# The opening loads of a fused attention and feed-forward kernel: batch 0's state block in one load with the first half of x, the first quarter of w_in as whole blocks, its stores issued by GpSimd

## The chip, the cores and the metric

The kernel runs on one core of one Trainium2 chip. The metric is the device time of one execution in microseconds (us). Three executions of the kernel before took 629.32, 629.43 and 630.81 us, so the median is 629.43 us. TensorE is called PE here, VectorE DVE, ScalarE ACT, GpSimd POOL and SyncE SP.

## The reference

Eight batches of eight heads attend between 512 rows of x and 32 rows of a state, in both directions. The result, 4608 rows of 512 numbers, goes through a feed-forward block whose activation is `h - tanh(h)`.

```python
scores = scale * x @ state.T;  a = softmax(scores);   xread = a @ state
scores2 = scale * state @ x.T; a2 = softmax(scores2); sread = a2 @ x
rows = concatenate([xread, sread])         # B, H, 544, 64 -> 4608 rows of 512
h = rows @ w_in                            # 512 x 2048
out = (h - tanh(h)) @ w_out                # 2048 x 512
```

The inputs x, state, `w_in` and `w_out` arrive as numpy arrays. The two weights are 64-bit floats: the kernel loads them as pairs of 32-bit words and makes 32-bit floats of them on the chip. The rest is 32-bit.

## The kernel before

**Stages.** Work goes chunk by chunk, one chunk for each batch and a last one for the state rows. Within a chunk the hidden layer is made in 16 slices of 128 columns, and each slice is multiplied with its rows of `w_out`. The product state times `w_in` is taken first (called m in the code), so that the attention weights can be multiplied with m directly and the read of the state needs no step of its own. Batch 0 has a hand-written opening, which is what the change touches. The others come from generators that a list of due steps drives.

**The opening.** Its order is written out in the string `SEQ` (line 821): each token is one step, and `tc.keep_in_program_order` holds the steps of an engine in this order. The steps that matter here:

- `D`: a matmul of zeros on PE (line 720). Five stand at the start.
- `S0`, `S1` (line 724): the scores of half 0 and half 1 of x for batch 0. Two matmuls each, of the state block with the two column groups of that half.
- `c0`, `c1` (line 729): ACT copies the scores out of PSUM. `T0`, `T1` (line 735): PE transposes them.
- `M0`, `B0`, `E0`, `Z0`, `z0`, `q0`, `N0` (lines 738 to 753): the softmax of half 0, all on DVE but the exponential `E0` on ACT. `A0` (line 758) transposes the result back on PE.
- `bj`, `aj`, `rj`, `pj` (lines 136 to 139): the four steps that turn a weight block from 64 into 32 bits. `b` and `a` run on DVE, `r` on ACT, `p` on DVE again. j counts the four blocks of the first quarter of `w_in` (tiles w00 to w03), each 128 columns wide, then two row blocks of `w_out`.
- After `pj` of the first four blocks, the converted block is stored to the buffer `wf` in device memory (line 777), from which the other batches read it much later.
- `mj` multiplies block j with the state of batches 0 and 1, `hj` and `Hj` are the first hidden slices.

DVE's order begins `b0 a0 M0 B0 p0 Z0 b1 a1 z0 p1 q0 a2 b2 N0 p2`.

**The loads.** SP issues nearly all transfers, in the order of the program, on one queue (q1 in the profile). Before the first step the code issues: `x00`, the state block with the first column group of half 0 (128 rows of 3 KB); from ACT, on a second queue (q10), the second column group of half 0 (128 rows of 2 KB); then from SP w00, half 1 of x, `sps` (another layout of the state, 256 KB), w01, w02, w03 and two blocks of `w_out`. Each further weight block is loaded when a conversion frees its buffer; that is `load(1)` in the step `p`. The blocks w00 to w03 are 128 columns of all 512 rows of `w_in`: a row of the tile is four pieces of 1 KB from four places.

The lines with which the opening sets its loads up:

```python
xb = big("x00", [P, 768], F32)
xrs = [pool.tile([P, 2, 512], F32, tag="x", name=f"xT0{hf}", bufs=XB) for hf in range(2)]
nc.sync.dma_start(xb, x0)
nc.scalar.dma_start(xrs[0][:, 1], xT[0, 0][:, 1])
load(1)
nc.sync.dma_start(xrs[1], xT[0, 1])
nc.sync.dma_start(sps, sp[0])
load(4)
```

`pooled(dst, src)` (line 300) issues a transfer from GpSimd, in the order of such calls. GpSimd's queue otherwise begins its transfers at 87.67 us, with the reads of `wf`.

Of the kernel before, what the change touches and what calls it, by code (L numbers as in the profile page):

```python
# [20 lines left out]
P = 128  # L21
# [4 lines left out]
NQ = 4  # L26
# [9 lines left out]


@with_exitstack
def attention_ffn(ctx: ExitStack, tc: tile.TileContext, xT, xn, x0, bh, sp, sm, win, wout, xout, tout, sout):

# [54 lines left out]
    def big(name, shape, dtype):  # L97
        return pool.tile(shape, dtype, tag="big", name=name, bufs=BIG)
# [7 lines left out]
    class Weight:  # L106
# [2 lines left out]
        def __init__(self, src, name):  # L109
            self.src, self.name = src, name  # L110

        def load(self):
            if self.src.dtype == F32:
                self.raw = next(raws)(f"{self.name}d", [P, 512], F32)
                dst = self.raw
            else:
                self.raw = next(raws)(f"{self.name}d", [P, 512, 2], U32)
                dst = self.raw.rearrange("p f w -> p (f w)")
            src = self.src.bitcast(dst.dtype)
            if len(src.shape) == 3:  # L120
                dst = dst.rearrange("p (r f) -> p r f", r=4)
            loadlog.append(nc.sync.dma_start(dst, src).ins)

        def steps(self, dst):

# [516 lines left out]
    def advance(units, n=1):  # L642
# [5 lines left out]


    w0 = [  # L650
        [Weight(win[r * P : r * P + P, 512 * q : 512 * q + 512], f"w{q}{r}") for r in range(DM // P)]
        for q in range(NQ)
    ]

    w0[0] = [
        Weight(win[:, j * P : j * P + P].rearrange("(r p) f -> p r f", p=P), f"w0{j}") for j in range(4)
    ]
    wos = [Weight(wout[f * P : f * P + P], f"wo{f}") for f in range(NFF)]
    wfs = {}

    def convert_win(q, p):
        if p % 2 == 0:
            wfs[q, p // 2] = pool.tile([P, 2, 512], F32, tag="wf", name=f"w0{q}{p // 2}", bufs=WB)
        made = w0[q][p].convert(wfs[q, p // 2][:, p % 2])
        if p % 2:
            nc.sync.dma_start(wf[q][:, p - 1 : p + 1], wfs[q, p // 2])
        return made
# [22 lines left out]

    aTs[0] = pool.tile([P, 2, 2, 512], F32R, tag="aT0", name="aT0", bufs=1)
    sps = pool.tile([P, 4, P], F32, tag="sm", name="sps", bufs=1)
    xb = big("x00", [P, 768], F32)
    xrs = [pool.tile([P, 2, 512], F32, tag="x", name=f"xT0{hf}", bufs=XB) for hf in range(2)]
    nc.sync.dma_start(xb, x0)
    nc.scalar.dma_start(xrs[0][:, 1], xT[0, 0][:, 1])
    load(1)
    nc.sync.dma_start(xrs[1], xT[0, 1])
    nc.sync.dma_start(sps, sp[0])
    load(4)  # L700
    bdr = xb[:, :256].rearrange("p (i m) -> p i m", i=4)
    moving = {(0, 0): xb[:, 256:]} | {(j, c): xrs[j][:, c] for j, c in ((0, 1), (1, 0), (1, 1))}

    warm = bank(ps_a, "warm")
    m_first[0] = pool.tile([P, 2, 512], F32, tag="mr", name="mr00", bufs=RRB)
# [11 lines left out]
    def step(op):  # L717
        k, j = op[0], int(op[1]) if len(op) > 1 else 0
        if k == "D":
            o(nc.tensor.matmul(warm[:, :256], blank[:, :P], blank, start=True, stop=True))  # L720
        elif k == "S":
            sps_ps[j] = bank(ps_o, f"sps0{j}")
            for c in range(2):
                o(nc.tensor.matmul(sps_ps[j][64 * c : 64 * c + 64], bdr[:, 2 * j + c], moving[j, c], start=True, stop=True))
        elif k == "c":
            if j == 0:
                kept[0] = pool.tile([P, 2, 512], F32, tag="g", name="s0", bufs=GB)
            ss[j] = kept[0][:, j]
            o(nc.scalar.copy(ss[j], sps_ps[j]))
        elif k == "T":  # L730

            tps[j] = bank(ps_o, f"tps0{j}")
            for t in range(4):
                cols = slice(P * t, P * t + P)
                o(nc.tensor.transpose(tps[j][:, cols], ss[j][:, cols], ident))
        elif k == "M":
            ms[j] = pool.tile([P, 16, 1], F32, tag="m1", name=f"m10{j}")
            o(nc.vector.reduce_max(ms[j], tps[j].rearrange("p (a n) -> p a n", n=32), axis=AX.X))
        elif k == "B":
            es[j] = pool.tile([P, 512], F32, tag="e", name=f"e0{j}")  # L740
            s3 = tps[j].rearrange("p (a n) -> p a n", n=32)
            o(nc.vector.tensor_sub(e3(j), s3, ms[j].broadcast_to([P, 16, 32])))
        elif k == "E":
            o(nc.scalar.activation(es[j], es[j], AF.Exp, scale=SCALE))
        elif k == "Z":
            zs[j] = pool.tile([P, 16, 1], F32, tag="z", name=f"z0{j}")
            o(nc.vector.reduce_sum(zs[j], e3(j), axis=AX.X))
        elif k == "z":
            o(nc.vector.tensor_scalar_add(zs[j], zs[j], EPS))
        elif k == "q":  # L750
            o(nc.vector.reciprocal(zs[j], zs[j]))
        elif k == "N":
            o(nc.vector.tensor_mul(e3(j), e3(j), zs[j].broadcast_to([P, 16, 32])))
        elif k == "A":
            aps[j] = bank(ps_o, f"aps0{j}")
            for t in range(4):
                cols = slice(P * t, P * t + P)
                o(nc.tensor.transpose(aps[j][:, cols], es[j][:, cols], ident))
        elif k == "y":
            ats[j] = pool.tile([P, 512], F32, tag="p2t", name=f"at0{j}", bufs=PTB)  # L760
            o(nc.scalar.copy(ats[j], aps[j]))
        elif k in "abrp":
            if j not in csteps:
                if j > 3:
                    if j == 4:
                        plain[0] = big("wp0", [P, 2, DM], F32)
                    csteps[j] = wos[j - 4].steps(plain[0][:, j - 4])
                else:
                    if j % 2 == 0:
                        wb[j // 2] = pool.tile([P, 2, 512], F32, tag="wf", name=f"w00{j}", bufs=WB)  # L770
                    csteps[j] = w0[0][j].steps(wb[j // 2][:, j % 2])
            o(csteps[j]["abrp".index(k)]())
            if k == "p":
                load(1)
            if k == "p" and j < 4:
                w = wb[j // 2][:, j % 2].rearrange("p (r f) -> p r f", r=4)
                nc.sync.dma_start(wf[0][:, :, j * P : j * P + P], w)
        elif k == "m":
            w = wb[j // 2][:, j % 2].rearrange("p (r f) -> p r f", r=4)
            if j >= APART:  # L780
                mps[j] = bank(MP[j], f"mps0{j}").rearrange("p (r f) -> p r f", r=4)
                for p in range(4):
                    o(nc.tensor.matmul(mps[j][:, p], sps[:, p], w[:, p], start=True, stop=True))
                return

            mps[j] = bank(MP[j], f"mps0{j}").rearrange("p (b k f) -> p b k f", b=2, k=2)
            for p in (0, 2):
                for b in range(2):
                    for c in range(2):
                        rows = slice(64 * c, 64 * c + 64)  # L790
                        cols = slice(64 * b, 64 * b + 64)
                        o(nc.tensor.matmul(mps[j][rows, b, p // 2], sps[:, p + c, cols], w[:, p + c], start=True, stop=True))
        elif k in "kR":
            b = "kR".index(k)
            if b and 0 not in m_second:
                m_second[0] = second(0)
            cols = slice(j * P, j * P + P)
            if j < APART:
                o(nc.scalar.copy((m_first, m_second)[b][0][:, :, cols], mps[j][:, b]))
                return  # L800
            for c in range(2):
                rows = slice(64 * c, 64 * c + 64)
                o(nc.scalar.copy((m_first, m_second)[b][0][rows, :, cols], mps[j][64 * b : 64 * b + 64, c::2]))
        elif k in "hH":
            if k == "h":
                hps[j] = bank(ps_h if j > 1 else ps_o, f"hps0_{j}")
            i = "hH".index(k)
            o(nc.tensor.matmul(hps[j], m_first[0][:, i, j * P : j * P + P], ats[i], start=(i == 0), stop=(i == 1)))  # L808
        elif k == "X":
            t = hts[j] = pool.tile([P, 512], F32, tag="t", name=f"t0_{j}", bufs=TB)  # L810
            hts[j, 0] = nc.scalar.activation(t, hps[j], AF.Tanh)
            o(hts[j, 0])
        elif k == "x":
            g = chunks[0].g[j] = pool.tile([P, 512], F32, tag="g", name=f"g0_{j}", bufs=GB)
            d = nc.vector.tensor_sub(g, hps[j], hts[j])
            o(d)
            tanhs.append((hts[j, 0].ins, d.ins))
# [9 lines left out]
    turn = firstDVE[0]  # L827
    for p in range(2):
        with tc.issue_after(turn):
            turn = convert_win(1, p)  # L830
        load(1)
        m_first_two(1, p)

# [510 lines left out]
```

## Time and profile before

| what | value |
|---|---|
| median of three executions | 629.43 us |
| the profiled execution | 629.0 us |
| its span, first to last instruction | 627.2 us |
| around the span | 1.8 us |
| PE busy | 621.5 us, 99% |
| DVE, ACT, POOL busy | 78%, 59%, 6% |
| granted PE clock over the span | 0.999 |
| bytes moved | 155.9 MB, mean 249 GB/s |

The share of busy time is a mean over the whole span. PE's 99% contain the matmuls of zeros of the opening and matmuls whose modelled end includes a wait, so the first 14 us have to be read by themselves: by the chain that ended last, the waits and the order of time.

### The profile page before, as it was taken

The numbers are of one execution on the slowest core, as the hardware profiler recorded it, in microseconds if no ns is written. First come the engines' busy times: TensorE is split into PE (matmuls) and PEld (weight loads), VectorE is DVE, ScalarE is ACT, GpSimd is POOL, SyncE is SP. The second block draws the span as 40 slices with busy tenths as digits, with TensorE's granted clock in tenths as the row PEclk, the third lists the DMA queues.
The fourth block names the chain that finished last, engine by engine and source line by source line (L and its number), as shares of the span: only waits on it lengthen the run. The fifth ranks groups of instructions, "written<-read, shape, count | busy, mean of one in ns | idle before, by whom it ended". The sixth has DMA issues, their size and how long they took to land.

```text
span 627.2 us, 9849 instructions
## 1 busy us (share of the span) xinstructions
PE 621.5 (99%) x3610; PEld 490.9 (78%) x3610; DVE 488.8 (78%) x781; ACT 370.4 (59%) x613; POOL 38.7 (6%) x66
## 2 busy tenths in 40 slices
PE   8999999999999999999999999999999999999997
PEld 5456677788888788778886678788888888888997
DVE  5999998799697696998357679988955878764582
ACT  5876777678666475755346785447555543562642
POOL 0000002132311000000000000000000000010000
PEclk9999999999999999999999999999999999999999
DMA  9993875869988857999716996765555675699990
GB/s 318 354 390 135 302 245 145 256 194 341 291 278 287 280 177 262 319 315 397 253 34 217 338 345 212 228 209 168 176 168 183 201 187 164 201 260 341 410 337 26
DMA packets 68672, 155.90 MB, mean 249 GB/s; under 512 B 6032, under 2 KB 27920, under 8 KB 68624
## 3 DMA queue, kind: packets, MB, share of 16 engines
q1 hardware_dynamic: 62400, 134.04, 63.7%
q0 software_dynamic: 6080, 20.98, 11.5%
q8 instruction: 28, 0.46, 0.3%
q10 hardware_dynamic: 144, 0.26, 0.1%
q14 instruction: 20, 0.16, 0.1%
HBM read 110.69 MB, written 44.56 MB: 248 GB/s over the span
## 4 chain that ended last, share of the span: by engine, by line
PE 96%; DVE 2%; ACT 1%; issue 0%; ACTq 0%
PE X L1067 14%; PE hps L553 10%; PE hps L554 10%; PE hps L555 10%; PE ops L606 8%; PE ops L608 8%; PE ops L607 8%; PE Y0m L1067 5%; PE Y1m L1067 5%; PE mps L263 2%; PE mps L179 2%; PE X L1173 2%; PE ops L604 2%; PE Y8m L1173 1%; PE rps L501 1%; PE hps L808 1%
## 5 line engine op out<-in xcount | busy, mean ns | idle before, releaser
L606 PE MATMUL ops<-wo,g 128*128 128x512 f32 x244 | 95.5, 396 | 0.0
L607 PE MATMUL ops<-wo,g 128*128 128x512 f32 x244 | 95.2, 390 | 0.0
L553 PE MATMUL hps<-aT,m 128*128 128x512 f32 x240 | 94.7, 397 | 0.0
L554 PE MATMUL hps<-aT,m 128*128 128x512 f32 x240 | 93.8, 391 | 0.1
L555 PE MATMUL hps<-aT,m 128*128 128x512 f32 x240 | 93.8, 391 | 0.0
L608 PE MATMUL ops<-wo,g 128*128 128x512 f32 x244 | 88.3, 393 | 0.0
L568 ACT ACTIVATE t<-hps 128x512 f32<-128x512 f32 x64 | 38.4, 601 | 57.9 <-PE hps L555 57.2
L568 DVE TENSOR_TENSOR G<-hps,t 128x512 f32<-128x512 f32 x64 | 43.8, 687 | 36.8 <-ACT t L568 36.7
L606 PEld LDWEIGHTS ops<-wo,g 128*128 128x128 f32 x244 | 45.7, 188 | 15.6 <-issue 1.9
L553 PEld LDWEIGHTS hps<-aT,m 128*128 128x128 f32 x240 | 45.0, 188 | 14.5 <-issue 2.5
L580 DVE TENSOR_TENSOR t<-hps,t 128x512 f32<-128x512 f32 x61 | 41.7, 683 | 18.4 <-ACT t L580 18.0
L104 ACT CAST g<-t 128x512 fp32r<-128x512 f32 x61 | 37.8, 619 | 28.5 <-DVE t L580 27.9
L608 PEld LDWEIGHTS ops<-wo,g 128*128 128x128 f32 x244 | 45.6, 188 | 10.8 <-DVE wo L104 0.8
L555 PEld LDWEIGHTS hps<-aT,m 128*128 128x128 f32 x240 | 45.0, 188 | 11.0 <-issue 1.7
L607 PEld LDWEIGHTS ops<-wo,g 128*128 128x128 f32 x244 | 45.8, 188 | 9.9 <-DVE wo L104 0.3
L554 PEld LDWEIGHTS hps<-aT,m 128*128 128x128 f32 x240 | 45.1, 188 | 9.7 <-DVE aT L104 0.5
L580 ACT ACTIVATE t<-hps 128x512 f32<-128x512 f32 x61 | 36.4, 597 | 26.3 <-PE hps L555 25.9
L1067 PE MATMUL X<-g0m,W0m 128*128 128x512 f32 x192 | 47.9, 390 | 0.0
L104 DVE TENSOR_TENSOR g<-t,g 128x512 fp32r<-128x512 f32 x61 | 41.6, 684 | 7.1 <-ACT g L104 6.9
L1067 PE MATMUL X<-g1m,W1m 128*128 128x512 f32 x192 | 45.8, 389 | 0.0
L104 ACT CAST g1m<-G 128x1024 fp32r<-128x1024 f32 x28 | 29.2, 1056 | 27.6 <-PE Y1m L1067 10.9
L1067 PEld LDWEIGHTS X<-g0m,W0m 128*128 128x128 f32 x192 | 36.0, 188 | 8.3 <-issue 0.8
(279 smaller groups left out, 1155.4 us busy)
## 6 DMA issues: line engine op xcount, KB each, us to landing
w<-wf POOLq DMA_DIRECT2D x32, 256.0 KB, 6.5
mm<-st POOLq DMA_DIRECT2D x16, 512.0 KB, 6.3
xn<-in_xn SPq DMA_DIRECT2D x16, 512.0 KB, 5.8
mr<-mm SPq DMA_DIRECT2D x16, 512.0 KB, 5.1
wsd<-ws SPq DMA_DIRECT2D x16, 512.0 KB, 7.7
wod<-wo SPq DMA_DIRECT2D x32, 256.0 KB, 6.6
W0m<-wsd SPq DMA_DIRECT2D x16, 512.0 KB, 3.7
W1m<-wsd SPq DMA_DIRECT2D x16, 512.0 KB, 3.9
```

The lines of the kernel that those rows point to most:

```text
L104: return nc.scalar.copy(hi, src), (sub or nc.vector).tensor_sub(lo, src, hi)
L179: made = nc.tensor.matmul(pss[b][rows], sp2[r, p + c, 64 * b + at : 64 * b + at + 32], w[r, c], start=True, stop=True,)
L553: nc.tensor.matmul(ps, mhi[k][:, cols], ahi[:, k], start=(k == 0), stop=False)
L554: nc.tensor.matmul(ps, mhi[k][:, cols], alo[:, k], start=False, stop=False)
L555: made = nc.tensor.matmul(ps, mlo[k][:, cols], ahi[:, k], start=False, stop=(k == nk - 1))
L568: main(nc.scalar.activation(t, ps, AF.Tanh), nc.vector.tensor_sub(g, ps, t))
L580: tanhs.append((nc.scalar.activation(t, ps, AF.Tanh).ins, nc.vector.tensor_sub(t, ps, t).ins))
L606: nc.tensor.matmul(o, g[:, 0, tok], w[:, 0], start=(f in self.begins), stop=False)
L607: nc.tensor.matmul(o, g[:, 0, tok], w[:, 1], start=False, stop=False)
L608: return nc.tensor.matmul(o, g[:, 1, tok], w[:, 0], start=False, stop=stop).ins
L1067: made = nc.tensor.matmul(out[t], w[:, e, x, cols], y[:, e], start=first and j == 0 and e == 0 and c == 0, stop=last and j == 3 and e == 1 ...
L1173: made = nc.tensor.matmul(out, o[:, x, s], w[:, y], start=first and jp == 0 and s == 0 and c == 0, stop=last and jp == 1 and s == 3 and c ...
```

## The change

It alters four things in the opening, all of them in what is loaded and stored and by which queue.

1. `x00` becomes one tile of 128 rows of 5 KB: the state block and both column groups of half 0. It is loaded by one transfer from SP. The transfer of the second column group from ACT is gone. The tile lies in the buffer `aT1` instead of in one of the sixteen `big` ones, and one buffer of the kind `x` stays free.
2. The first quarter of `w_in` comes as an input of its own, `w0b`, laid out in four whole blocks on the host. A load of w00 to w03 is now 128 rows of 4 KB. The rest of `w_in` is an array of 1536 columns.
3. w00 is issued by ACT instead of by SP, as ACT's first instruction.
4. The four stores of the converted blocks to `wf` are issued by GpSimd with `pooled` instead of by SP.

The scores of half 1 take a PSUM bank of another pool. The code also gains a branch for a step of index 6, which begins the next quarter's first block early; the string `SEQ` is the same as before and names no such step, so nothing takes that branch.

```diff
-        def load(self):
+        def load(self, queue=nc.sync):
...
-            loadlog.append(nc.sync.dma_start(dst, src).ins)
+            loadlog.append(queue.dma_start(dst, src).ins)
...
-    w0[0] = [
-        Weight(win[:, j * P : j * P + P].rearrange("(r p) f -> p r f", p=P), f"w0{j}") for j in range(4)
-    ]
+    w0[:0] = [[
+        Weight(w0b[j], f"w0{j}") for j in range(4)
+    ]]
...
-    xb = big("x00", [P, 768], F32)
-    xrs = [pool.tile([P, 2, 512], F32, tag="x", name=f"xT0{hf}", bufs=XB) for hf in range(2)]
+    xb = pool.tile([P, 1280], F32, tag="aT1", name="x00", bufs=1)
+    xr = pool.tile([P, 2, 512], F32, tag="x", name="xT01", bufs=XB)
     nc.sync.dma_start(xb, x0)
-    nc.scalar.dma_start(xrs[0][:, 1], xT[0, 0][:, 1])
-    load(1)
-    nc.sync.dma_start(xrs[1], xT[0, 1])
+    next(loads).load(nc.scalar)
+    nc.sync.dma_start(xr, xT[0, 1])
...
-            sps_ps[j] = bank(ps_o, f"sps0{j}")
+            sps_ps[j] = bank((ps_o, ps_h)[j], f"sps0{j}")
...
-                nc.sync.dma_start(wf[0][:, :, j * P : j * P + P], w)
+                pooled(wf[0][:, :, j * P : j * P + P], w)
...
-    x0 = c(np.concatenate([bd[0].reshape(P, 256), xT[0, 0, :, 0]], axis=1))
+    x0 = c(np.concatenate([bd[0].reshape(P, 256), xT[0, 0].reshape(P, 2 * S)], axis=1))
...
+    w0b = c(win[:, :512].reshape(4, P, 4, P).transpose(2, 1, 0, 3).reshape(4, P, 512))
+    win = c(win[:, 512:])
```

What the two programs issue at the start, on SP (an arrow points from what is read to what is written; `in_x` are the inputs of x, `in_w` is `w0b`, `wf` the store of a converted block). Before:

```order
L695 DMA x_101<-in_x 128x768
L122 DMA w00d<-in_win 128x4x256
L698 DMA xT_103<-in_xT 128x1024
L699 DMA sps<-in_sp 128x512
L122 DMA w01d<-in_win 128x4x256
L122 DMA w02d<-in_win 128x4x256
L122 DMA w03d<-in_win 128x4x256
L122 DMA wo0d<-in_wout 128x1024
L122 DMA wo1d<-in_wout 128x1024
L122 DMA w10d<-in_win 128x1024
L777 DMA wf_95<-w_125 512x1x128
L122 DMA w11d<-in_win 128x1024
```

SP after:

```order
L693 DMA x_101<-in_x 128x1280
L695 DMA xT_102<-in_xT 128x1024
L696 DMA sps<-in_sp 128x512
L120 DMA w01d<-in_w 128x1024
L120 DMA w02d<-in_w 128x1024
L120 DMA w03d<-in_w 128x1024
L120 DMA wo0d<-in_wout 128x1024
L120 DMA wo1d<-in_wout 128x1024
L120 DMA w10d<-in_win 128x1024
L120 DMA w11d<-in_win 128x1024
```

The first load grew from 768 to 1280 words a row, w00 is gone from behind it, and the store of the first block no longer stands between w10 and w11.

On ACT, before, from its first instruction:

```order
L696 DMA xT_102<-in_xT 128x512
L729 ACT_TABLE_LOAD
L729 COPY s_133<-sps_128 128x512
L138 ACTIVATE w00r<-w00d 128x512
L744 ACTIVATE e_147<-e_147 128x512
```

ACT after:

```order
L120 DMA w00d<-in_w 128x1024
L726 ACT_TABLE_LOAD
L726 COPY s_131<-sps_126 128x512
L136 ACTIVATE w00r<-w00d 128x512
L741 ACTIVATE e_145<-e_145 128x512
```

ACT issues w00 in the place where it issued the second column group of x; its other instructions stand as before.

On GpSimd, before, from the making of the identity matrix to the first reads of `wf`:

```order
masks.py:197 MEMSET ident 128x128
masks.py:199 ISA
masks.py:199 AFFINE_SELECT ident<-ident 128x128
L246 DMA w_1023<-wf_95 64x2x512 x2
L246 DMA w_1063<-wf_95 64x2x512 x2
```

GpSimd after:

```order
masks.py:197 MEMSET ident 128x128
masks.py:199 ISA
masks.py:199 AFFINE_SELECT ident<-ident 128x128
L305 DMA wf_95<-w_123 512x1x128 x2
L305 DMA wf_95<-w_181 512x1x128 x2
L244 DMA w_1021<-wf_95 64x2x512 x2
L244 DMA w_1061<-wf_95 64x2x512 x2
```

The four stores stand ahead of the reads of `wf`. On DVE and PE the two programs hold the same instructions in the same order; on PE both matmuls of `S0` now read the one tile `x00`.

## Rows read from the trace of the kernel before

**Rows 1.** The page: each engine's busy time, share of the span, instructions.

```profile
PE 621.5 (99%) x3610; PEld 490.9 (78%) x3610; DVE 488.8 (78%) x781; ACT 370.4 (59%) x613; POOL 38.7 (6%) x66
```

**Rows 2.** The chain that ended last, 0 to 14 us: start, length, what.

```profile
5.31 1.16 PE sps L724 x4
...
7.23 0.64 PE tps L735 x4
...
7.90 0.70 DVE m L738
...
13.02 0.58 DVE e L753
...
13.73 0.30 PE aps L758
```

**Rows 3.** Busy time by stretch: start:end, length, each engine's busy time (instructions), clock.

```profile
12.00:14.00 2.00, 1.36 (x19) 1.15 (x20) 2.00 (x6) 1.24 (x2) 0.00 (x0) 1.00 1.05 402
14.00:16.00 2.00, 2.00 (x14) 1.46 (x13) 2.00 (x5) 2.00 (x6) 0.00 (x0) 1.00 1.01 392
```

**Rows 4.** Waits for transfers, 0 to 40 us: total, times, longest.

```profile
DVE w00r L137 <- DMA w00d<-in_win: 7.0, 1, 7.0
...
ACT w03r L138 <- DMA w03d<-in_win: 0.7, 1, 0.7
...
PEld sps L724 <- DMA x<-in_x: 0.6, 1, 0.6
```

**Rows 5.** The opening in order of time: start, length, engine, line, operation.

```profile
0.74 0.40 ACTq L696 DMA_DIRECT2D xT<-in_xT  x1
...
5.24 0.64 PE L724 MATMUL sps<-x 128*64 128x512 f32 x1
...
5.39 0.64 PE L724 MATMUL sps<-xT,x 128*64 128x512 f32 x1
...
6.99 0.47 DVE L137 TENSOR_SCALAR w00r<-w00d 128x512 uint16<-128x512 uint16 x1 [6.99 <-DMA w00d<-in_win]
...
7.35 0.41 DVE L136 TENSOR_SCALAR w<-w00d 128x512 uint32<-128x512 uint32 x1
...
10.01 0.69 DVE L747 TENSOR_REDUCE z<-e 128x16 f32<-128x512 f32 x1
...
10.61 0.46 DVE L137 TENSOR_SCALAR w01r<-w01d 128x512 uint16<-128x512 uint16 x1
...
12.12 0.25 DVE L751 RECIPROCAL z<-z 128x16 f32<-128x16 f32 x1
12.23 0.54 SPq L777 DMA_DIRECT2D wf<-w  x1
...
23.59 0.41 DVE L136 TENSOR_SCALAR w<-w10d 128x512 uint32<-128x512 uint32 x1
```

**Rows 6.** Packets by queue, 3 to 4 us: packets, MB, share of 16 engines.

```profile
q1 hardware_dynamic: 74, 0.21, 58.1%
q10 hardware_dynamic: 72, 0.14, 42.5%
```

**Rows 7.** All packets, 5 to 6 us and then 6 to 7 us.

```profile
DMA packets 273, 0.36 MB, mean 363 GB/s; under 512 B 9, under 2 KB 243, under 8 KB 273
DMA packets 140, 0.40 MB, mean 398 GB/s; under 512 B 15, under 2 KB 34, under 8 KB 140
```

**Rows 8.** Stores from SP, 0 to 30 us: count, size, median us from issue to landing.

```profile
wf<-w SPq DMA_DIRECT2D x4, 256.0 KB, 7.7
```

**Rows 9.** GpSimd's transfers, by form: busy us in all, mean ns to issue one.

```profile
L246 POOL DMA_DIRECT2D w<-wf x32 | 19.2, 606 | 127.9 <-DMA smr<-in_sm 86.4 <-DVE wst L249 41.4
L266 POOL DMA_DIRECT2D mm<-st x16 | 11.7, 734 | 48.7 <-ACT st L228 48.7
```

**Rows 10.** DVE beside GpSimd's first transfers, in order of time.

```profile
87.67 1.32 POOL L246 DMA_DIRECT2D w<-wf  x2 [86.36 <-DMA smr<-in_sm]
...
88.39 0.42 DVE L136 TENSOR_SCALAR wor<-wo13d 128x512 uint32<-128x512 uint32 x1
```

More of the change, by code (lines that the diff above doesn't have):

```diff
@@ L38, in attention_ffn @@
 @with_exitstack
-def attention_ffn(ctx: ExitStack, tc: tile.TileContext, xT, xn, x0, bh, sp, sm, win, wout, xout, tout, sout):
+def attention_ffn(ctx: ExitStack, tc: tile.TileContext, xT, xn, x0, bh, sp, sm, w0b, win, wout, xout, tout, sout):
     nc = tc.nc
@@ L119, in load @@
             src = self.src.bitcast(dst.dtype)
-            if len(src.shape) == 3:
-                dst = dst.rearrange("p (r f) -> p r f", r=4)
-            loadlog.append(nc.sync.dma_start(dst, src).ins)
+            loadlog.append(queue.dma_start(dst, src).ins)
         def steps(self, dst):
@@ L650, in attention_ffn, with convert_win @@
     w0 = [
-        [Weight(win[r * P : r * P + P, 512 * q : 512 * q + 512], f"w{q}{r}") for r in range(DM // P)]
-        for q in range(NQ)
-    ]
-    w0[0] = [
-        Weight(win[:, j * P : j * P + P].rearrange("(r p) f -> p r f", p=P), f"w0{j}") for j in range(4)
-    ]
+        [Weight(win[r * P : r * P + P, 512 * q - 512 : 512 * q], f"w{q}{r}") for r in range(DM // P)]
+        for q in range(1, NQ)
+    ]
+    w0[:0] = [[
+        Weight(w0b[j], f"w0{j}") for j in range(4)
+    ]]
     wos = [Weight(wout[f * P : f * P + P], f"wo{f}") for f in range(NFF)]
     wfs = {}
-    def convert_win(q, p):
-        if p % 2 == 0:
+    def convert_win(q, p, begun=None):
+        if p % 2 == 0 and begun is None:
             wfs[q, p // 2] = pool.tile([P, 2, 512], F32, tag="wf", name=f"w0{q}{p // 2}", bufs=WB)
-        made = w0[q][p].convert(wfs[q, p // 2][:, p % 2])
+        made = begun[3]().ins if begun else w0[q][p].convert(wfs[q, p // 2][:, p % 2])
         if p % 2:
@@ L701, in attention_ffn @@
     bdr = xb[:, :256].rearrange("p (i m) -> p i m", i=4)
-    moving = {(0, 0): xb[:, 256:]} | {(j, c): xrs[j][:, c] for j, c in ((0, 1), (1, 0), (1, 1))}
+    moving = {(0, c): xb[:, 256 + 512 * c : 768 + 512 * c] for c in range(2)} | {(1, c): xr[:, c] for c in range(2)}
     warm = bank(ps_a, "warm")
@@ L763, in step @@
             if j not in csteps:
-                if j > 3:
-                    if j == 4:
+                if j == 6:
+                    wfs[1, 0] = pool.tile([P, 2, 512], F32, tag="wf", name="w010", bufs=WB)
+                    csteps[j] = w0[1][0].steps(wfs[1, 0][:, 0])
+                elif j > 3:
+                    if 0 not in plain:
                         plain[0] = big("wp0", [P, 2, DM], F32)
@@ L829, in attention_ffn @@
         with tc.issue_after(turn):
-            turn = convert_win(1, p)
+            turn = convert_win(1, p, csteps.get(6) if p == 0 else None)
         load(1)
@@ L1327 @@
     win, wout = (c(w).view(np.int64) if w.dtype == np.float64 else w for w in (moe_w_in, moe_w_out))
+    w0b = c(win[:, :512].reshape(4, P, 4, P).transpose(2, 1, 0, 3).reshape(4, P, 512))
+    win = c(win[:, 512:])
     nc = bacc.Bacc("TRN2", target_bir_lowering=False, num_devices=1, dynamic_dma_scratch_size=1024)
-    arrays = {"in_xT": xT, "in_xn": xn, "in_x0": x0, "in_bh": bh, "in_sp": sp, "in_sm": sm, "in_win": win, "in_wout": wout}
+    arrays = {"in_xT": xT, "in_xn": xn, "in_x0": x0, "in_bh": bh, "in_sp": sp, "in_sm": sm, "in_w0": w0b, "in_win": win, "in_wout": wout}
     args = [
```

## The prediction

> **What bounds the kernel now.** I read the page first. PE is busy 621.5 us, 99% of the span [rows 1], so only what makes PE start its real work sooner or later can move the end. Next comes the chain that ended last, for the first 14 us, because the change touches nothing but the loads and stores there. The reader is to see four stations in it [rows 2]: PE at the zeros until 5.31 us and then at the scores S0 (`sps`), their transposition T0 (`tps`) at 7.23, then from 7.90 to 13.6 a run that is nearly all DVE, from the row maximum M0 to the normalised weights N0, and at 13.73 PE's transposition A0 (`aps`). The busy time by stretch says what limits each part [rows 3]: between 12 and 14 us DVE is busy 2.00 of 2 us and PE 1.36, and from 14 to 16 PE is busy 2.00 of 2 as well. So DVE, working without a pause from M0 on, sets when PE gets A0, and PE, full from there on, carries any shift to the end. I take it that a microsecond at M0 is a microsecond of the kernel.
>
> What sets M0? The waits name it [rows 4]: in the first 40 us an engine waits for a transfer five times (three of them stand there), always in the opening: PE for x (0.6 us), DVE for w00, PE for half 1 of x, ACT for w02 and for w03 (0.7 us). In order of time [rows 5] two branches end almost together. S0's second operand is there at 5.39, ACT copies the scores, PE transposes them, and M0 starts at 7.90, that is **2.51 us after S0 has all its input** (7.90 - 5.39). Beside it w00 lands at 6.99 and DVE does its two conversion steps until 7.35 + 0.41 = 7.76. Neither branch has more than 0.15 us to spare.
>
> **The change part by part.**
>
> *The load of x.* Before, S0 needed 128 rows of 3 KB from SP's queue and 128 of 2 KB from ACT's, 0.39 and 0.26 MB. The two queues were served one for one: between 3 and 4 us 74 packets went on q1 and 72 on q10, in bytes 0.21 to 0.14 MB, the ratio of the row sizes [rows 6]. After the change S0 needs 128 rows of 5 KB from SP (0.655 MB), and on ACT's queue stand not rows of x but 128 rows of 4 KB of w00 (0.52 MB), which S0 doesn't need. If the queues still alternate, x is complete only when nearly as many rows of w00 have gone. Taking 7 of 8, moved by then is 0.655 + 0.46 = 1.11 MB, where it was 0.39 + 0.23 = 0.62 MB: 0.49 MB more. Where the engines are full they move 0.363 to 0.398 MB in a microsecond [rows 7], so x lands some 1.2 to 1.35 us later. Longer rows should go a little faster than those of 1 KB that fill much of the first of these two stretches, so I take the short end, 1.2 us. S0 starts at 5.24 + 1.2 = 6.44 instead of having its input at 5.39, and M0 at 6.44 + 2.51 = 8.95 instead of 7.90: **+1.05 us**. Bounds: at best S0's input, 0.65 MB as before, lands at 5.39 as before or a little sooner, and M0 gains at most the 0.14 us by which DVE's other branch ended ahead of it (7.90 - 7.76): -0.15. At worst x lands together with w00, which moved the same 1.15 MB in all by 6.99 before: 6.99 + 2.51 - 7.90 = +1.6.
>
> *w00 as a whole block, by ACT.* It is issued at 0.74, in the place of the load of x that ACT issued [rows 5]. The same bytes have to land before both branches are served, so w00 comes at about 6.7 or sooner, and its two DVE steps end by 7.5, hidden behind M0 at 8.95. If x were early instead, this branch would set M0 again. I cost it at 0.
>
> *w01 to w03 as whole blocks.* They can end ACT's waits for w02 and w03, 0.7 us for the latter [rows 4]. These are ACT's, whose steps DVE picks up later without waiting: DVE is full there [rows 3]. With DVE a microsecond later still, the cover grows. 0.
>
> *The stores by GpSimd.* SP loses four issues of half a microsecond and the waits ahead of them, and later loads of weights go out sooner. After 14 us no engine waits for a load [rows 4], so nothing is gained: 0. What waits for the stores is the next block's conversion, which overwrites the buffer that the first two read from, at 23.59 [rows 5]. Before, the second store went out at 12.23 and took 7.7 us [rows 8], done by 19.9, with 3.7 us to spare. Now it goes out some 1 us later, as does the conversion. To issue it GpSimd needs longer than SP: 64 rows cost it 606 ns and 128 rows 734 [rows 9]; at the 128 ns for 64 rows between these, 512 pieces cost about 0.73 + 6 x 0.128 = 1.5 us. That leaves 2 us of the cover. Should the store be later still, DVE would stand at that conversion for the rest. GpSimd's own queue is empty until 87.67 us [rows 10], so nothing stands behind the stores.
>
> *The buffers.* x00 now lies where batch 1's weights come later, long after S0 has read it. 0.
>
> **The sum.** +1.05 us, all of it from S0 waiting for x. The profiled execution took 629.0 us, the span and 1.8 us around it, so it would take 630.05; the median of the three runs is 0.43 above it, which gives **630.5 us**, 0.17% more. About 0.3% (1.9 us) is what a measurement of this kernel can tell from no change, so this would read as no change.
>
> **The rivals.**
>
> *x is drained first.* If each transfer engine finished its rows of x before it turned to w00, S0's input would land where it did, M0 would start at 7.75 to 7.90, and the time would be 629.3 to 629.4 us, no change at all. For it: x starts first on its queue. Against it: the one-for-one count while both queues still held rows [rows 6]. The Trainium skill, "DMA: Bandwidth & Descriptors", section "Queues, rings and completion order", says that an engine takes turns between queues a whole packet at a time and that a packet typically holds 9 to 17 descriptors; if an engine's eight rows of x made one such packet, this rival would be the case, and by that rule the sum would be 0. Here the rows of the two queues alternate, so the trace speaks against that size of packet for these loads.
>
> *The load doesn't do what it says.* A row of 5 KB may move as two pieces, since no load of the kernel before has rows above 4 KB, and the trace shows none to compare with. With x in twice as many packets, w00 lands first and x last, with all 1.15 MB moved: +1.6 us by the bound above, 631.0 us.
>
> *GpSimd holds DVE: slower.* While GpSimd writes the descriptors of a store, DVE's conversion steps `a` could stand still. The store of w00 has Z0 and b1 behind it on DVE, 0.69 + 0.46 us of cover, and then a1; that of w01 has only q0, 0.25 us, and then a2 [rows 5]; those of w02 and w03 have more than 1.5 us of other work. At 1.5 us a store that is 0.35 + 1.25 = 1.6 us at most, on the chain that sets A0. With the +1.05 it gives 632.1 us, 0.4% slower; it decides from the point where DVE loses more than 0.85 us in all. For it: DVE has no pause there. Against it: the one such step beside an issue of GpSimd, at 88.39, took 0.42 us [rows 10], and 0.41 where GpSimd was idle [rows 5]. The Trainium skill, "SBUF — State Buffer", section "SBUF: two separate sides", says that DVE in a two-port mode and GpSimd lock each other out for a whole instruction, and warns of GpSimd transfers beside DVE for that reason. It would put the price at up to the 1.6 us above; the pair of rows shows no such stall, but it is one pair.
>
> **How the numbers follow.** The forecast has 0.70 (629.9 to 631.1 with its bounds and the spread of the runs), x drained first 0.13, the split row 0.07, GpSimd's hold 0.07, and 0.03 are for what I don't see. The forecast and the first two rivals all lie within 0.3%, as does half of what remains. Faster by over 0.3% would need M0 almost 2 us sooner, at 6.0, before w00 has even landed; only the unseen can give that: 0.03. Slower by over 0.3% is GpSimd's hold and a share of the unseen: 0.08. Within 0.3%: 0.89. For 8 times in 10 the range reaches from x drained first with a little of the spread, 629.0, to the lower part of GpSimd's hold, 631.6.
>
> **What would show it.** In the profile after: S0 on PE at 6.2 to 6.7 us, M0 1.0 us later than 7.90, and the same 5.8 us from M0 to A0 (13.73 - 7.90). S0 at 5.4 would mean that x is drained first; S0 at 7 with w00 landed before it, a split row. If the stretch from M0 to A0 grows, with pauses ahead of a1 or a2, GpSimd holds DVE. DVE waiting at the conversion of w10 would mean that a store is late. The prediction would be wrong as a whole if the chain behind A0 took up a microsecond somewhere, or if PE's granted clock, 1.00 through the opening [rows 3], fell while PE waits longer for S0.

## The result, and the profile after

The changed kernel takes 633.15 us, the median of 6 runs (632.35 to 634.64); the kernel before, on the same chip, 629.97 (6 runs, 628.7 to 631.0). The ratio is **1.0055, 95% interval 1.0042 to 1.0067**: slower by some 3.2 us, where 630.5 was predicted and 631.6 was the upper end of the range. The profiled execution of after is the slowest of its six, 634.64 us with a span of 632.8.

From the page of after, the busy times; [rows 1] has them before:

```profile
PE 623.6 (99%) x3610; PEld 490.0 (77%) x3610; DVE 488.6 (77%) x781; ACT 369.6 (58%) x613; POOL 42.1 (7%) x70
```

PE's busy time grew by 2.1 us, the span by 5.6 (from 627.2): most of the loss in this execution is time in which PE does nothing. The chain of after in order of time (start, length, what), beside [rows 2]:

```profile
0.74 5.22 DMA x<-in_x
6.01 1.10 PE sps L721 x4
...
8.53 0.70 DVE m L735
...
14.36 0.63 PE aps L755 x4
...
27.50 7.17 DMA wf<-w
34.85 0.43 DVE w L134
```

Up to A0 the picture is the one predicted, only smaller: S0 waits for x, M0 starts at 8.53 instead of 7.90, and A0 comes 5.83 us after M0 (14.36 - 8.53), as before (13.73 - 7.90). The new link is the second last: a *store* of a converted block lies on the chain for 7.17 us, and a conversion on DVE waits for it. Among the waits of the first 40 us (engine, line, what it waited for: total, times, longest) stands:

```profile
DVE w L134 <- DMA wf<-w: 3.9, 1, 3.9
```

DVE stands 3.9 us for a transfer of `wf`, a wait that the kernel before doesn't have. In order of time, on DVE (start, length, line, operation, and in brackets the idle time before it and what ended it), first after:

```profile
24.07 0.42 DVE L134 TENSOR_SCALAR w<-w10d 128x512 uint32<-128x512 uint32 x1
...
30.29 0.71 DVE L104 TENSOR_TENSOR wo<-wor,wo 128x512 fp32r<-128x512 f32 x1
34.85 0.43 DVE L134 TENSOR_SCALAR w<-w12d 128x512 uint32<-128x512 uint32 x1 [3.85 <-DMA wf<-w]
```

and w12's conversion before:

```profile
30.42 0.42 DVE L136 TENSOR_SCALAR w<-w12d 128x512 uint32<-128x512 uint32 x1
```

The conversion of w10, which [rows 5] has at 23.59 and which the prediction named as the one that could wait, comes at 24.07 without a wait. It is the next pair's, w12's, that stands: before it began at 30.42, right behind its neighbour. It overwrites the buffer that the third and the fourth store read. The four stores on GpSimd, and the last conversion steps of w01 and w03 on DVE:

```profile
10.86 1.40 POOL L305 DMA_DIRECT2D wf<-w  x1 [9.56 <-DVE w L137]
16.94 0.73 POOL L305 DMA_DIRECT2D wf<-w  x1 [4.68 <-DVE w L134]
23.14 0.71 POOL L305 DMA_DIRECT2D wf<-w  x1 [5.46 <-issue]
27.50 0.72 POOL L305 DMA_DIRECT2D wf<-w  x1 [3.65 <-DVE w L137]
```

```profile
12.14 0.69 DVE L137 CUSTOM_DVE_ANT_0 w<-w,w01r 128x1024 uint16<-128x1024 uint16 x1
...
16.82 0.69 DVE L137 CUSTOM_DVE_ANT_0 w<-w,w03r 128x1024 uint16<-128x1024 uint16 x1
```

w01 is ready at 12.83, but its store goes out at 16.94; w03 is ready at 17.51, and its store goes out at 27.50, ten microseconds late, and lands at 34.67. The names that the view gives for these idle times can't be right: DVE had long been done, and "issue" means that the profile shows nothing. What the stores do follow is one another. The view of transfers, asked for a short window around each issue, has for the four in their order, from issue to landing in us (last number):

```profile
wf<-w POOLq DMA_DIRECT2D x1, 256.0 KB, 5.8
...
wf<-w POOLq DMA_DIRECT2D x1, 256.0 KB, 5.9
...
wf<-w POOLq DMA_DIRECT2D x1, 256.0 KB, 4.1
...
wf<-w POOLq DMA_DIRECT2D x1, 256.0 KB, 7.2
```

The first three land at 16.7, 22.8 and 27.2 us, and the next store goes out about 0.3 us behind each, also where the landing was quicker (4.1 us). That is the theory which the runs below test: **each store is issued only when the one before it has landed.**

Why the wait reaches the end is read from the busy times by stretch (window, length, then PE, PEld, DVE, ACT, POOL busy, PE's granted clock, DMA share, GB/s):

```profile
24.00:30.00 6.00, 6.00 (x15) 2.65 (x15) 6.00 (x14) 4.32 (x9) 0.72 (x1) 1.00 0.84 282
30.00:36.00 6.00, 6.00 (x35) 3.15 (x34) 2.15 (x6) 3.34 (x5) 0.00 (x0) 1.00 0.99 397
36.00:42.00 6.00, 4.21 (x26) 1.55 (x25) 6.00 (x13) 2.54 (x4) 0.00 (x0) 1.00 0.87 270
```

DVE is busy all 6 us ahead of the wait and all 6 behind it: it has no slack in which to make the pause good. PE works on through the pause and stands idle for 1.79 us of the next six. Before, PE and DVE were busy 6.00 of 6 us in all three stretches; the last of them:

```profile
36.00:42.00 6.00, 6.00 (x45) 2.41 (x44) 6.00 (x15) 5.26 (x9) 0.00 (x0) 1.00 1.02 410
```

### The profile page after: what moved, and what is told of

Same layout as the page of the kernel before. It is cut to its first block, busy times and chain, and to the rows that moved or that the text cites. A ratio compares the mean times of both kernels' runs of the same rounds, so it can differ in the third digit from the quotient of the medians.

```text
span 632.8 us, 9845 instructions
## 1 busy us (share of the span) xinstructions
PE 623.6 (99%) x3610; PEld 490.0 (77%) x3610; DVE 488.6 (77%) x781; ACT 369.6 (58%) x613; POOL 42.1 (7%) x70
## 4 chain that ended last, share of the span: by engine, by line
PE 85%; DVE 5%; DMA 5%; ACT 3%; issue 1%; DVEq 0%; ACTq 0%; SPq 0%
PE X L1067 13%; PE hps L551 9%; PE hps L552 9%; PE hps L553 9%; PE ops L604 8%; PE ops L606 8%; PE ops L605 8%; PE Y1m L1067 5%; PE Y0m L1067 5%; PE mps L261 2%; PE X L1173 2%; PE Y8m L1173 1%; PE rps L499 1%; PE mps L177 1%; DMA mm<-st 1%
```

## The experiments

The stores' theory has two ways to be tested: give GpSimd's transfers more room in the program's setting that reserves memory for them (1024 in both kernels), and put the stores elsewhere. The rival is that GpSimd's stores are slow or disturbed in themselves, or that the loss comes from the load of x.

**e1: after, with twice the room.**

```diff
-    nc = bacc.Bacc("TRN2", target_bir_lowering=False, num_devices=1, dynamic_dma_scratch_size=1024)
+    nc = bacc.Bacc("TRN2", target_bir_lowering=False, num_devices=1, dynamic_dma_scratch_size=2048)
```

> The changed kernel with twice the memory that the program reserves for GpSimd's transfers (2048 instead of 1024 bytes a partition). Theory A (only one store of 512 pieces fits into that memory at a time, so each next store is issued only when the one before has landed): the four stores go out at about 10.9, 12.9, 14.9 and 17.6 us, right behind their conversions; the last has landed by 25, DVE no longer waits for it at 30.4, and the time falls from 633.15 to 630.5 us (+0.5 against before). Theory B (DVE's own accesses hold up GpSimd, or a store of 512 pieces simply takes GpSimd 6 us): the stores go out at 10.9, 16.9, 23.1 and 27.5 us as in the changed kernel, DVE waits 3.9 us, 633 us.

Measured: 629.45 us (10 runs), before on the same chip 629.25 (25 runs), ratio 1.0004, interval 0.9992 to 1.0016. The stores on GpSimd, and w12's conversion on DVE:

```profile
10.78 1.41 POOL L305 DMA_DIRECT2D wf<-w  x1 [9.48 <-DVE w L137]
13.08 0.76 POOL L305 DMA_DIRECT2D wf<-w  x1 [0.89 <-DVE z L748]
15.04 0.93 POOL L305 DMA_DIRECT2D wf<-w  x1 [1.20 <-DVE w L137]
17.87 0.72 POOL L305 DMA_DIRECT2D wf<-w  x1 [1.90 <-DVE w L137]
```

```profile
30.83 0.42 DVE L134 TENSOR_SCALAR w<-w12d 128x512 uint32<-128x512 uint32 x1
```

No other instruction differs from after, and the loss is gone. The second and the fourth store now go out 0.3 and 0.4 us after their blocks are ready (at 12.76 and 17.45 in this run), and the wait ahead of w12 has vanished. The third goes out at 15.04, while the first is still under way (it lands 5.8 us after 10.78), so three are under way at a time.

**e6: the dose between.** As e1, with 1536.

> The changed kernel with 1536 bytes a partition reserved instead of 1024. Theory A counted out: at 1024 one store fits at a time, at 2048 all went out behind their conversions. If the room goes by bytes, two stores fit at 1536: the second goes out near 13 us, the third only when the first has landed (near 17 us, instead of 15 at 2048), the fourth near 18 to 20; no wait of DVE, 629 to 630 us. If 1024 was only just short of some fixed need of the machinery, all four go out behind their conversions, at 10.8, 13, 15 and 17.9 us.

One run, 629.12 us. The stores:

```profile
10.76 1.40 POOL L305 DMA_DIRECT2D wf<-w  x1 [9.45 <-DVE w L137]
13.04 0.76 POOL L305 DMA_DIRECT2D wf<-w  x1 [0.89 <-DVE z L748]
17.04 0.72 POOL L305 DMA_DIRECT2D wf<-w  x1 [3.24 <-DVE w L134]
19.28 1.56 POOL L305 DMA_DIRECT2D wf<-w  x1 [1.51 <-DVE e L750]
```

Now the second goes out at once and the third waits, till 17.04, 6.3 us after the first went out; so does the fourth, 6.2 us after the second. The first two land 6.0 and 5.9 us after their issue, and again the store that waits goes out 0.3 us behind a landing. Two are under way at a time. So one at 1024, two at 1536, no store held up at 2048: the room is the cause, and a store of 512 pieces fills more than half of the 1024. With two at a time the fourth is early enough, and DVE has no wait for `wf`.

**e2: after, with the stores back on SP.**

```diff
-                pooled(wf[0][:, :, j * P : j * P + P], w)
+                nc.sync.dma_start(wf[0][:, :, j * P : j * P + P], w)
```

> The changed kernel with its four stores issued by SP again, in the places where they were before; the loads stay as changed. Both theories of the stores: DVE's wait of 3.9 us for the store is gone, M0 stays at 8.5 us (0.63 later than before), 630.4 us, +0.5 against before. If instead the loads were to blame, the time stays near 633.

Measured: 629.7 us (10 runs), ratio 1.0002, interval 0.9992 to 1.0013. With the other three parts of the change in place the loss is gone too, so none of them holds it. S0 and M0:

```profile
5.90 1.08 PE L721 MATMUL sps<-x 128*64 128x512 f32 x4 [0.52 <-DMA x<-in_x]
...
8.42 0.69 DVE L735 TENSOR_REDUCE m<-tps 128x16 f32<-128x512 f32 x1 [1.59 <-PE tps L732]
```

The delay of S0 is the same kind as in after (6.01 and 8.53), so it belongs to the load and not to the stores.

**e3: before, with the stores alone on GpSimd.** The same edit the other way round, in the kernel before.

> The kernel before with only the four stores moved to GpSimd; the loads are as before. Both theories of the stores: M0 at 7.9 us as before, the stores go out at about 10, 16, 22 and 27 us, DVE waits some 3 to 4.5 us at the conversion that follows 30 us, and the time is 2.5 to 4 us above before: 632.5 to 634. If GpSimd's stores only hurt together with the new loads, it stays at 630.

Measured: 635.6 us (4 runs, 634.45 to 638.65), ratio 1.0101, interval 1.0068 to 1.0135, more than expected. The stores and w12:

```profile
10.22 1.39 POOL L307 DMA_DIRECT2D wf<-w  x1 [8.92 <-DVE w L139]
17.26 0.74 POOL L307 DMA_DIRECT2D wf<-w  x1 [5.64 <-DVE w L139]
23.66 1.27 POOL L307 DMA_DIRECT2D wf<-w  x1 [5.66 <-DVE g L815]
29.74 0.72 POOL L307 DMA_DIRECT2D wf<-w  x1 [4.81 <-DVE g L104]
```

```profile
37.43 0.43 DVE L136 TENSOR_SCALAR w<-w12d 128x512 uint32<-128x512 uint32 x1 [6.78 <-DMA wf<-w]
```

This one part makes the kernel slower by more than the whole change does. The stores stand 7.0, 6.4 and 6.1 us apart instead of 6.1, 6.2 and 4.4, and DVE's wait is 6.78 us instead of 3.85. Each still follows the landing of the one before by 0.3 us (they take 6.7, 6.1 and 5.8 us to land); why the landings take longer here isn't settled. A second loss follows the wait, in the stretches behind it:

```profile
36.00:39.00 3.00, 0.51 (x2) 0.00 (x0) 1.57 (x5) 0.00 (x0) 0.00 (x0) 1.00 0.04 14
39.00:46.00 7.00, 5.12 (x23) 2.74 (x24) 7.00 (x15) 3.47 (x6) 0.00 (x0) 0.51 0.94 279
```

PE was busy 0.51 of 3 us, and from 39 to 46 its granted clock was 0.51 (1.00 again from 46 to 52), the lower of its two levels (1.2 instead of 2.4 GHz). DVE is busy 7.00 of those 7 us, so it isn't shown that the clock cost time there. Over e3's four runs the mean clock was 0.994 to 0.999, and the run with 0.999 is still 5.2 us above before (634.45): most of the loss doesn't go with the clock.

**e8: e3 with the room of 2048.**

> The kernel before with its four stores issued by GpSimd, as in e3_only_pool_stores, and 2048 bytes reserved. Theory A: the whole loss of 6.3 us of that run came from the missing room; DVE's wait of 6.8 us is gone, M0 stays at 7.9, 629.0 to 629.6 us, the same as before. If GpSimd's transfers slow the loads beside them, 630 us or more.

Measured: 630.14 us (10 runs), before 629.4 (19 runs), ratio 1.0013, interval 1.0003 to 1.0024. The fourth store:

```profile
17.35 0.72 POOL L307 DMA_DIRECT2D wf<-w  x1 [1.91 <-DVE w L139]
```

It went out at 29.74 in e3, and no wait of DVE for `wf` is left. About 5.6 of e3's 6.3 us go with the room. The other 0.7 us (0.13%) are more than theory A allowed, and 630.14 lies on the side of its rival, that GpSimd's transfers slow what runs beside them. In this profile w12's conversion comes at 30.48, 0.06 us later than before, so the opening doesn't show the 0.7 us; e1, with the same stores and the same room, equals before. Whether GpSimd's stores cost a tenth of a per cent by themselves stays open.

**e5: only the first two stores on GpSimd**, the other two on SP, in after.

```diff
-                pooled(wf[0][:, :, j * P : j * P + P], w)
+                (pooled if j < 2 else nc.sync.dma_start)(wf[0][:, :, j * P : j * P + P], w)
```

> The changed kernel with only the first two stores issued by GpSimd and the last two by SP; the reserved memory stays at 1024 bytes. Theory A (one store at a time): the second store still goes out only behind the landing of the first, near 17 us, and lands near 22.5, ahead of the conversion at 24.1 that needs its buffer; DVE doesn't wait, 629.7 us (+0.4 against before). If GpSimd's stores cost by themselves, whatever their number, half of the loss stays: 631 us or more.

Measured: 630.25 us (10 runs), ratio 1.0012, interval 1.0003 to 1.0022.

```profile
10.78 1.40 POOL L305 DMA_DIRECT2D wf<-w  x1 [9.47 <-DVE w L137]
16.69 0.74 POOL L305 DMA_DIRECT2D wf<-w  x1 [4.51 <-DVE w L134]
```

The second store still waits for the first, till 16.69, 3.5 us later than the prediction reckoned; it lands 5.8 us after that, at 22.5, ahead of w10's conversion at 23.98, and DVE never waits for `wf`. So the delay of one store is covered; it is the queue of four that isn't. The time lies between theory A's 629.7 and the rival's 631, and as in e8 a tenth of a per cent is left without a wait that explains it.

**e4 and e7: the load of x alone at first.** After, with the stores on SP as in e2 and w00 issued by SP behind x, so that nothing stands on ACT's queue. e7 is e4 a second time.

```diff
-    next(loads).load(nc.scalar)
+    load(1)
```

> The changed kernel with its stores on SP again and with w00 issued by SP behind x instead of by ACT. Theory of the queues (x came late because rows of w00 on ACT's queue took turns with it): S0 starts at 5.2 to 5.5 us instead of 6.0, w00 lands at 6.2 to 6.5, M0 at 7.7 to 8.0, 629.8 to 630.0 us, the same as before within 0.1 us. If x was late because of its 5 KB rows themselves: S0 stays at 6.0, M0 at 8.5, 630.5 us.

> The same kernel as e4_x_alone_first, profiled once more, since there the four passes of S0 took 0.89 to 1.12 us each instead of 0.59 to 0.64. Theory of the queues: S0 starts at 5.2 to 5.4 us again; where its passes take 0.6 us, M0 starts at 7.7 to 7.9 us and the opening is as early as before or 0.1 us earlier. If M0 stays at 8.5 with passes of 0.6 us, the row of 5 KB costs something of its own.

Measured: e4 629.56 us (10 runs), ratio 1.0001, interval 0.9985 to 1.0017; e7, one run, 629.78. S0 in e4, S0 in e7 and M0 in e7, a fence for each kernel:

```profile
5.31 1.81 PE L721 MATMUL sps<-x 128*64 128x512 f32 x4
```

```profile
5.32 1.31 PE L721 MATMUL sps<-x 128*64 128x512 f32 x4
...
8.08 0.69 DVE L735 TENSOR_REDUCE m<-tps 128x16 f32<-128x512 f32 x1 [1.29 <-PE tps L732]
```

With nothing beside it x is there by 5.31 at the latest, without a wait of PE for it: the 0.6 to 0.7 us by which S0 came later in after and e2 were the turns given to w00. But M0 missed what was expected (7.7 to 8.0) in both: S0's four passes lasted longer, 1.81 and 1.31 us in all against 1.08 in after, so nothing of the gain reached M0 in e4 (8.56) and part of it in e7 (8.08). What differs between two executions of one kernel is no effect of the change. Its cause is open: the granted clock reads 1.00 in both. The rival, that rows of 5 KB cost something of their own, fails for S0's start, and S0's passes over the same tile took 1.08 us in after and e2.

None of these is measurably faster than the kernel before; e1, e2 and e4 equal it.

## Why the prediction was wrong, point by point

**The stores by GpSimd: the step that failed.** The prediction priced them at 0, and put down as the reason that nothing stands behind the stores on GpSimd's queue. What stood behind each store was the next one. It compared one store, the second, with its user at 23.59, with 2 us to spare, and took the other three for no worse. Two errors lie in that. First, the rate: it took GpSimd to pass a store on as soon as it was issued, and only asked what one issue costs (bounded by 1.5 us; measured 1.40 for the first, 0.71 to 0.73 for the rest). The trace before had on GpSimd only transfers of 64 and 128 rows [rows 9], and of the smaller ones four went out without a pause:

```profile
98.07 2.37 POOL L246 DMA_DIRECT2D w<-wf  x4 [9.08 <-DVE wst L249]
```

They took 6.4 us each to land, in the median, so four were under way at once, with 1024 reserved and 256 KB each, as much as a store. What the stores have more of is pieces: 512 of 512 bytes instead of 64 rows of 4 KB. Whether GpSimd can have two transfers of 512 pieces under way was an unknown with no row, and it got no bound. Second, the last: a delay that repeats adds up to the last store, and its user, w12's conversion, wasn't looked at. With one store after the other's landing at the 7.7 us of [rows 8], the fourth would have gone out at about 11 + 3 x 7.7 = 34 and landed at 42, against 30.42: the bound from the rows would have been a loss of over 10 us, and the range would have reached the 3.2 us that were measured.

The text did name the sign, DVE waiting at a conversion because a store is late; it named the wrong conversion and gave it no price.

**The load of x: right mechanism, mis-sized.** The queues take turns one for one, as [rows 6] said. Packets of x (q1) and w00 (q10) in after between 3 and 4 us:

```profile
q1 hardware_dynamic: 48, 0.25, 58.8%
q10 hardware_dynamic: 45, 0.18, 44.7%
```

The bytes by packet are 5.2 and 4 KB: rows go whole, which rejects the split row, and alternate, which rejects that x is drained first. These counts are of all 16 engines together; the first turns are what engines give that each alternate. Up to 2.58 us, and from there to 2.79:

```profile
q1 hardware_dynamic: 16, 0.08, 25.2%
...
q10 hardware_dynamic: 16, 0.07, 106.6%
```

First 16 rows of x start and none of w00, then 16 of w00 and none of x: one row for each engine. (By the rule of the Trainium skill, "DMA: Bandwidth & Descriptors", section "Queues, rings and completion order", of 9 to 17 descriptors at a turn, eight rows an engine would have gone in one turn; these counts speak against it here.) S0 started at 6.01 instead of 6.44 and M0 at 8.53 instead of 8.95, so the term is +0.63 and not +1.05. The term that was off is the rate, and not only that of the 0.49 MB which the sum added: the bytes that it left to go as before went faster too. All packets from 3 to 5 us, first before, then after, a fence for each kernel:

```profile
DMA packets 456, 0.68 MB, mean 338 GB/s; under 512 B 32, under 2 KB 291, under 8 KB 456
```

```profile
DMA packets 187, 0.86 MB, mean 432 GB/s; under 512 B 0, under 2 KB 0, under 8 KB 187
```

By my estimate the 0.18 MB more of these two microseconds are 0.42 us at 432 GB/s, which is the size of the miss (1.05 - 0.63). w00 landed by 6.16 and its steps were done well ahead of M0, as costed.

**A microsecond at M0 is a microsecond of the kernel: not shown.** Of the 0.63 at M0, 0.48 is left at w10's conversion (24.07 - 23.59); in e1, where M0 comes 0.56 later than before (8.46), 0.41 is left at w12's (30.83 - 30.42). At the end e1 and e2 stand 0.2 to 0.45 us above before in their medians, with intervals that hold 1. That agrees with a small loss and can't be told from none.

**GpSimd hardly holds DVE.** M0 to A0 is 5.83 us in both kernels, and the conversion step of w01 that ran beside the first issue (at 11.6, within 10.86 to 12.26) took 409 ns, against 0.41 before [rows 5]. One step did get longer, z0, which ended together with that issue. First before, then after:

```profile
11.29 0.17 DVE L749 TENSOR_SCALAR z<-z 128x16 f32<-128x16 f32 x1
```

```profile
11.92 0.34 DVE L746 TENSOR_SCALAR z<-z 128x16 f32<-128x16 f32 x1
```

It took 0.33 to 0.34 us in all six profiles with that store on GpSimd and 0.17 to 0.18 in the four with it on SP; the step behind it came no later. The other way round the effect is larger: the store issues beside three or four such short steps (TENSOR_SCALAR) took GpSimd 1.27 to 1.56 us (the first in every run, e3's third, e6's fourth), those beside none 0.71 to 0.74. The Trainium skill, "SBUF — State Buffer", section "SBUF: two separate sides", warns of GpSimd's transfers beside DVE; the trace agrees in kind, with 0.17 us on DVE's side that cost nothing and up to 0.85 on GpSimd's, which e1 shows to be no part of the loss. This rival came nearest to the time, by another mechanism than the one that ran.

**The size of the loss.** From e1 to after only the room differs. w12's conversion comes 4.0 us later (34.85 - 30.83). Against the kernel before, measured beside each, after is 3.2 us slower and e1 0.2, a difference of 3.0 in the medians; the two profiled spans differ by 5.4, and after's is the slowest of its six runs. The rest of the latter isn't settled. ACT's waits for `mr`, over the whole span, differ too (10.3 us in after, 6.4 in e1), but whether they reach the end isn't shown.

## What to carry to other kernels

When transfers move to another queue, ask how many of them its issuer can have under way, and count their pieces against the memory that is reserved for it: an issue that costs under a microsecond says nothing of that. Check the cover of every transfer of the row, the last one's above all, since a delay that repeats adds up to it. And a load on a second queue isn't free beside an urgent one: here it took every second turn.

## What the runs showed of the hardware that was not expected

- The room reserved for GpSimd's transfers sets how many stores of 512 pieces of 512 bytes are under way: one at 1024, two at 1536, and at 2048 none was held up. Loads of 256 KB in 64 rows went out four at a time at 1024. The trace doesn't name the wait; it puts the time down to an engine that was done long ago, or to "issue".
- GpSimd's stores travel in larger packets than SP's. In the view of transfers from 10.5 to 17 us of after, in which one store moves, its queue has

```profile
q0 software_dynamic: 80, 0.26, 10.4%
```

  80 packets for 256 KB, that is above 3 KB each in the mean, though the pieces are 512 bytes. In e2, where SP issues the four stores, the same view from 10.5 to 26 us has 2048 packets between 512 bytes and 2 KB, one for each piece.
- GpSimd's issue of a store and short steps on DVE are longer beside each other: 1.27 to 1.56 us instead of some 0.72 for the issue, 0.34 instead of 0.17 for the step that ends with it.
- In e3 the granted clock fell to 0.51 for some 7 us behind 3 us in which PE had worked 0.51 us.
- The same four passes of S0 took 1.08, 1.31 and 1.81 us in three executions whose granted clock reads 1.00.
